# Linear attention with decay, then an MLP: three loads issued earlier, two groups of stores later, and a state sum moved ahead of the normalised rows

## The chip, the cores and the metric

One core of one Trainium2 chip. The metric is the device time in microseconds of one execution, as the median over several; lower is better. The engines are TensorE (PE; its weight loads are shown as PEld), VectorE (DVE), ScalarE (ACT), GpSimd (POOL) and SyncE (SP, which here only issues transfers; rows of an engine's queue carry a q, as in SPq).

## What is computed

Causal linear attention with a decay `lam` per head, in blocks of 64 positions with a running state, and on its output a layer norm and an MLP with a residual. The input is float32: q, k and v of 4 batches, 8 heads, 768 positions, 64 wide; the model width is 512, the hidden width 2048.

```python
for b in range(nb):                      # 12 blocks of 64 positions
    intra = einsum('bhic,bhjc->bhij', qb, kb) * Dmask[None]
    intra = einsum('bhij,bhjd->bhid', intra, vb)
    inter = einsum('bhid,bhde->bhie', qb * lam_pow[None], kv_state)
    out[:, :, sl] = intra + inter
    kv_state = lam_block * kv_state + einsum('bhsd,bhse->bhde', kb * rev_pow, vb)
xn = (x - mean(x)) / sqrt(var(x) + 1e-06) * g_ln     # x: heads side by side
out = x + maximum(xn @ w_ch1, 0.0) @ w_ch2
```

## The kernel before

**The pieces.** The 3072 rows (4 batches of 768) are cut into twelve *pairs* u = 0 to 11 of 256 rows; a pair is two chunks of 128 rows, piece of sequence u // 4 of batch u % 4. What the change calls the eighth pair is u = 7, and so on. Pairs 0 to 5 hold the score matrix of a whole chunk (functions `kv`, `scores`, `mask`, `av`), pairs 6 to 11 that of 64 positions (`kv64`, `scores64`, `mask64`, `states64`, `av64`).

**The way of one pair.** SP loads k, q and v (`load_in`, issued at L76 as one transfer for pairs below 6 and at L80 as two of 256 KB from pair 6 on). `in_k_one` (L231) casts k to bfloat16, `in_q_one` (L236) multiplies q by powers of lam, `in_v` (L242) does that to v; each `_one` call does half, on the engine that it is given. `transpose_dma` (L257) has the transposes of k and q made by a transfer that SP issues. PE makes the state terms pk (L324 or L389) and the scores (L279 or L370); DVE masks the scores (mA, L289 or L376). DVE adds pk to the old state (Stmp, L334, or Smid and Stmp, L405 and L408) and POOL multiplies the sum by the decay and writes the new state Sn (L330). PE multiplies scores by v (`av`, L436 or L423) and q by the state (`inter`, L449). `norm` reads the result: ACT copies it to x and takes its sum and mean (L475, L476), DVE writes the normalised rows x' (xc, L477). `to_xT` transposes x' for the MLP: on PE for pairs 2 to 4 (L510, copied by ACT at L511), else by a transfer from SP (L503). The MLP's first product is L547 (two chunks at once) or L658 (one), its relu on ACT (hT, L550 or L661). From group 4 on the second product is made with seven products in place of eight: DVE forms sums of hidden rows (`h_sums`: hs, L565 to L567) and the products go to four banks pwa to pwd (L582); they are scaled and added into x by ACT and POOL (L606 and L607, L614 and L615) and by DVE (L595). `rstd_of` is L520, L521 and L525; the earlier groups use L684 and L708. `store` (L716) writes a pair's rows in two transfers from SP.

**The two states of a pair.** `new_state(u, 0, ...)` adds pk0 to the batch's old state and has POOL make Sn; `new_state(u, 1, ...)` adds pk1 to that new Sn and has POOL make the next. So the second sum reads what POOL made of the first.

**What sets the order.** Nothing reorders the work: the program text is the schedule. Every engine runs its instructions in the order in which the text records them, and waits at an instruction for what it reads or overwrites. The MLP of earlier pairs is a list of units; `units(n)` records the next n of them between the steps of the attention. So the text from L1100 on is a long list of steps such as `load_in(8, "k", nc.sync)`, `units(1)`, `X(7)`. `Y(u)` and `X(u)` are pieces that hold pair u's state and scores beside pair u - 1's output; `Y` is called for pairs 4 and 5 (the fifth and sixth), `X` for 6 to 11. In `Y`, DVE's order before the change is: first sum, first mask, the two rows of x', second sum, three masks.

**Buffers.** PSUM has one tag "mm" of four banks, shared by pk, early scores, the MLP's first product and the second product's accumulators; a bank is free when its reader is done. k, q and v have three buffers each for what is loaded (inp), kq and its transposes three, vb four, x six; x is overwritten by the MLP's result and is free when its store has landed. SP's transfers share eight semaphores, so that each waits for the transfer eight before it.

Of the kernel before, what the change touches and what calls it, by code (L numbers as in the profile page):

```python
# [17 lines left out]
def kernel(  # L18
# [11 lines left out]
    nc = tc.nc  # L30
# [41 lines left out]
    def fill(got, name, u, hs, eng=None):  # L72
        eng = eng or nc.sync
        src = dict(k=k, q=q, v=v)[name]
        if u < LB:
            eng.dma_start(got[:, hs], source(src, u, hs))  # L76
            return
        cc, b = divmod(u, B)
        for j in range(2):
            eng.dma_start(got[:, hs, j * D:(j + 1) * D],  # L80
                          src[b, hs, cc * W + j * C:cc * W + (j + 1) * C, :].rearrange("h p d -> p h d"))
# [11 lines left out]
    def load_in(u, name, eng):  # L93
        got = qkv_in[u][name]
        fill(got, name, u, slice(0, H), eng)
        qkv_in[u][name] = got.rearrange("p h (j d) -> p h j d", j=2)
# [101 lines left out]
    def open_window(u):  # L198
        kq = wk.tile([128, 2, NP, 2, 2, D], BF16, tag="kq", bufs=3, name="kq")
        vb = wk.tile([128, H, 2, D], BF16, tag="vb", bufs=4, name="vb")  # L200
        st[u] = dict(kq=kq, vb=vb)
        if u < XB:
            st[u]["kqT"] = wk.tile([128, 2, NP, 2, 128], BF16, tag="kqT", bufs=3, name="kqT")

    def part(a, dst, hs):

        return dst[:, a, hs.start // 2:hs.stop // 2].rearrange("p a j e d -> p a e j d")
# [21 lines left out]
    def in_k_one(u, eng, j):  # L229
        src = qkv_in[u]["k"].rearrange("p (a e) j d -> p a e j d", e=2)  # L230
        (eng.copy if eng is nc.scalar else eng.tensor_copy)(part(0, st[u]["kq"], ALL)[:, :, :, j], src[:, :, :, j])  # L231

    def in_q_one(u, eng, j):
        src = qkv_in[u]["q"].rearrange("p (a e) j d -> p a e j d", e=2)
        lq = (lam_q[:, :, j] if u < LB else lam_p[:, 0, :]).rearrange("p (a e) -> p a e", e=2)
        eng.tensor_tensor(part(1, st[u]["kq"], ALL)[:, :, :, j], src[:, :, :, j],  # L236
                          lq[:, :, :, None].to_broadcast([128, NP, 2, D]), op=ALU.mult)

    def in_v(u, eng, hs=ALL):
        n = hs.stop - hs.start  # L240
        lv = lam_v[:, hs, :, None] if u < LB else lam_p[:, 1, hs, None, None]
        eng.tensor_tensor(st[u]["vb"][:, hs], qkv_in[u]["v"][:, hs], lv.to_broadcast([128, n, 2, D]), op=ALU.mult)  # L242
# [10 lines left out]
    def transpose_dma(u, a):  # L253
        s = st[u]
        if "kqT" not in s:
            s["kqT"] = wk.tile([128, 2, NP, 2, 128], BF16, tag="kqT", bufs=3, name="kqT")
        nc.sync.dma_start_transpose(s["kqT"][:, a].rearrange("p b j t -> p (b j) t"),  # L257
                                    s["kq"][:, a].rearrange("p b j e d -> p (b j e d)"))
# [26 lines left out]
    def mask(u, hf, heads=(0, 1)):  # L285
        s = st[u]
        kp = keep.rearrange("p a b t -> p a (b t)")
        for e in heads:
            nc.vector.tensor_tensor(s[f"mA{hf}"][:, e], s[f"sc{hf}"][e],  # L289
                                    kp[:, None, :, :].to_broadcast([128, 2, 2, 128]), op=ALU.mult)  # L290
# [38 lines left out]
    def decay(eng, dst, src):  # L329
        eng.tensor_tensor(dst, src, lam_s[:, :, None].to_broadcast([128, NP, D]), op=ALU.mult)  # L330

    def state_sum(u, ab):
        tmp = wk.tile([128, NP, D], F32, tag="Stmp", name="Stmp")
        nc.vector.tensor_tensor(tmp, st[u]["pk"][ab], state[u % B], op=ALU.add)  # L334
        return tmp

    def new_state(u, ab, eng):

        s = st[u]
        b = u % B  # L340
        if ab == 1 and len(s["pk"]) == 1:
            return
        old = state.get(b)
        if ab == 0:
            s["S"] = [(old, old)]
        Sn = wk.tile([128, NP, D], BF16, tag="S", bufs=12, name="Sn")
        if old is None and eng is nc.scalar:
            for p in range(NP):
                nc.scalar.activation(Sn[:, p], s["pk"][ab][:, p], ACT.Identity, scale=lam_s[:, p:p + 1])
        elif old is None:  # L350
            decay(nc.vector, Sn, s["pk"][ab])
        else:
            tmp = s.pop("tmp", None) or state_sum(u, ab)
            decay(eng, Sn, tmp)
        state[b] = Sn
        if ab == 0:
            s["S"].append((Sn, Sn))
# [97 lines left out]
    def reader(u, act=False):  # L455
        s = st[u]
        for ab in range(2):
            if s["S"][ab][1] is not None:
                seen = wk.tile([128, H], F32, tag="seen", name="seen")
                (nc.scalar.copy if act or u > WG else nc.vector.tensor_copy)(seen, s["po"][ab][:, :, 0])  # L460

    def norm(u, ab, early=False):
        s = st[u]
        po = s["po"][ab].rearrange("p h d -> p (h d)")
        if "x" not in s:
            s["x"] = xp.tile([128, 2, DM], F32, tag="x", bufs=6, name="x")
            s["mv"] = xp.tile([128, 2, 2], F32, tag="mv", name="mv")
            s["xc"] = wk.tile([128, 2, DM], BF16, tag="xc", name="xc")
        x, mv, xc = s["x"][:, ab], s["mv"][:, ab], s["xc"][:, ab]
        if u >= 2:  # L470
            if ab == 0:
                s["sum"] = xp.tile([128, 2], F32, tag="sum", name="sum")
                s["nmean"] = xp.tile([128, 2], F32, tag="nmean", name="nmean")
            sm, nm = s["sum"][:, ab:ab + 1], s["nmean"][:, ab:ab + 1]
            nc.scalar.activation(x, po, ACT.Copy, accum_out=sm)  # L475
            nc.scalar.activation(nm, sm, ACT.Copy, scale=-1.0 / DM)  # L476
            nc.vector.scalar_tensor_tensor(xc, in0=po, scalar=nm, in1=g_row, op0=ALU.add, op1=ALU.mult)  # L477
            return
        if not early:
            nc.scalar.copy(x, po)  # L480
        stats = wk.tile([128, 6], F32, tag="stats", name="stats")
        nc.vector.bn_stats(stats, po if early else x)
        nc.vector.bn_aggr(mv, stats)
        n_h = 2 if u == 0 else 1
        for h in range(n_h):
            sl = slice(h * DM // n_h, (h + 1) * DM // n_h)
            nc.vector.scalar_tensor_tensor(xc[:, sl], in0=po[:, sl], scalar=mv[:, 0:1], in1=g_row[:, sl],
                                           op0=ALU.subtract, op1=ALU.mult)
# [205 lines left out]
    def rows_of(u):  # L694

        cc, b = divmod(u, B)
        order = "(c p j) d -> j p c d" if u < LB else "(j c p) d -> j p c d"
        return out[b, cc * W:(cc + 1) * W, :].rearrange(order, c=2, j=2)
# [15 lines left out]
    def store(u):  # L714
        for j in range(2):
            nc.sync.dma_start(rows_of(u)[j], o_of[u][half[j]])  # L716
# [222 lines left out]
    def Y(u):  # L939
        kv(u)  # L940
        av(u - 1, range(NP))
        inter(u - 1, 0, fence=False)
        reader(u - 1, act=True)
        scores(u, 0)
        scores(u, 1, early=True)
        inter(u - 1, 1)
        new_state(u, 0, nc.gpsimd)
        mask(u, 0, (0,))
        norm(u - 1, 0)
        norm(u - 1, 1)  # L950
        new_state(u, 1, nc.gpsimd)
        mask(u, 1)
        mask(u, 0, (1,))

# [102 lines left out]
    def units(n):  # L1057
        for _ in range(n):
            f, *a = next(steps)
            f(*a)  # L1060
# [76 lines left out]
    load_in(6, "v", nc.sync)  # L1137
    units(1)
    Y(4)
    transpose_dma(5, 0)  # L1140
    transpose_dma(5, 1)
# [24 lines left out]
    open_in(8, False)  # L1166
    units(4)
    Y(5)
    transpose_dma(6, 1)
    units(1)  # L1170
    in_q_one(7, nc.gpsimd, 0)
    units(1)
# [6 lines left out]
    rstd_of(4)  # L1179
    units(2)  # L1180
    in_k_one(7, nc.vector, 1)
    load_in(7, "v", nc.sync)
    load_in(8, "k", nc.sync)
    in_v(7, nc.gpsimd)
    units(1)
    in_k_one(7, nc.scalar, 0)
# [2 lines left out]
    units(1)  # L1189
    X(6, rest=False)  # L1190
    open_window(8)
    store(1)
    store(2)
    transpose_dma(7, 0)
    transpose_dma(7, 1)
    to_xT(5, 0)
    to_xT(5, 1)
    units(3)
# [2 lines left out]
    open_in(9, False)  # L1201
    units(1)
    in_k_one(8, nc.gpsimd, 0)
    units(2)
    in_k_one(8, nc.vector, 1)
    units(1)
    load_in(8, "q", nc.sync)
    load_in(8, "v", nc.sync)
    units(1)
    rstd_of(5)  # L1210
    units(3)
    units(1)
    X(7)
    in_q_one(8, nc.gpsimd, 0)
    in_q_one(8, nc.gpsimd, 1)
    load_in(9, "k", nc.sync)
    units(1)
    in_v(8, nc.gpsimd)
    units(1)
# [33 lines left out]
    transpose_dma(9, 0)  # L1253
    to_xT(7, 1)
    units(2)
    store(3)
    units(2)
    m2s[6].sums(0, 4)
    m2s[6].sums(4, 8)
    units(3)  # L1260
    store(4)
    load_in(10, "q", nc.sync)
    units(3)
    rstd_of(7)
    units(1)
# [114 lines left out]
```

## Time and profile before

| | us |
|---|---|
| median of 3 runs (lowest, highest) | 209.29 (208.67, 210.65) |
| the profiled execution | 209.5 |
| its span, first to last instruction | 207.8 |
| granted TensorE clock over it | 1.00 |
| ACT busy, share of the span | 122.5, 59% |
| POOL busy, share of the span | 84.9, 41% |

The span is that of one execution; 1.7 us of its time lie around it. Times in the text such as "at 69.53" are microseconds from the start of the span. In a row of groups or of the timeline, `out<-in` names what an instruction writes and reads, a number in brackets at the end is how long its engine had been idle before it, and the name behind the arrow what ended that. A row of waits gives the sum in us, the number of waits and the longest. The shares of the transfer engines by fortieths of the span:

```
DMA  4999999999899799999698789899999020058403
```

Each digit is a slice of 5.2 us, in tenths: the transfer engines are busy nearly throughout until about 160 us.

### The profile page before, as it was taken

The numbers are of one execution on the slowest core, as the hardware profiler recorded it, in microseconds if no ns is written. First come the engines' busy times: TensorE is split into PE (matmuls) and PEld (weight loads), VectorE is DVE, ScalarE is ACT, GpSimd is POOL, SyncE is SP. The second block draws the span as 40 slices with busy tenths as digits, with TensorE's granted clock in tenths as the row PEclk, the third lists the DMA queues.
The fourth block names the chain that finished last, engine by engine and source line by source line (L and its number), as shares of the span: only waits on it lengthen the run. The fifth ranks groups of instructions, "written<-read, shape, count | busy, mean of one in ns | idle before, by whom it ended". The sixth has DMA issues, their size and how long they took to land.

```text
span 207.8 us, 7500 instructions
## 1 busy us (share of the span) xinstructions
PE 197.0 (95%) x3229; PEld 159.8 (77%) x3229; DVE 137.5 (66%) x274; ACT 122.5 (59%) x284; POOL 84.9 (41%) x117
## 2 busy tenths in 40 slices
PE   1999999999999999997999999999999999999992
PEld 0588888454775686686888899887888888888881
DVE  3588451647875665859979874748877957865253
ACT  3787678435443575774575775584596575652630
POOL 5657059118674604535248361753265202002020
PEclk9999999999999999999999999999999999999999
DMA  4999999999899799999698789899999020058403
GB/s 111 301 252 221 183 266 169 200 293 270 214 201 284 180 159 216 175 229 233 110 236 123 167 179 168 181 256 131 210 165 203 6 51 3 17 122 276 148 6 97
DMA packets 91011, 36.41 MB, mean 175 GB/s; under 512 B 65121, under 2 KB 88161, under 8 KB 90978
## 3 DMA queue, kind: packets, MB, share of 16 engines
q1 hardware_dynamic: 86368, 31.53, 72.9%
q0 software_dynamic: 4224, 4.19, 12.9%
q8 instruction: 25, 0.41, 0.9%
q10 hardware_dynamic: 386, 0.20, 0.4%
q14 instruction: 8, 0.07, 0.1%
HBM read 27.27 MB, written 6.29 MB: 162 GB/s over the span
## 4 chain that ended last, share of the span: by engine, by line
PE 47%; DMA 27%; DVE 9%; POOL 8%; SPq 3%; issue 2%; ACT 1%; POOLq 0%; DVEq 0%; ACTq 0%
PE pm L547 20%; DMA w<-in_moe_w_ch_dram 11%; DMA qin<-in_q_dram 6%; PE pwd L582 5%; DMA kin<-in_k_dram 5%; PE pwc L582 5%; DMA vin<-in_v_dram 5%; PE pwa L582 5%; PE pm L684 3%; PE pm1t L658 3%; POOL vb L242 3%; DVE hs L567 2%; PE pwb L582 2%; DVE hs L565 2%; DVE x L595 2%
## 5 line engine op out<-in xcount | busy, mean ns | idle before, releaser
L547 PE MATMUL pm<-xT,w 128*128 128x256 bf16 x640 | 73.7, 273 | 0.2 <-DVE Stmp L334 0.2
L547 PEld LDWEIGHTS <-w 128*128 128x128 bf16 x640 | 61.4, 98 | 8.6 <-DVE Stmp L334 0.7
L550 ACT ACTIVATE hT<-pm 128x512 f16<-128x512 f32 x80 | 47.0, 597 | 25.1 <-PE pm L547 24.6
L684 PE MATMUL pm<-w,hT 128*128 128x512 f16 x128 | 29.6, 379 | 0.0
L582 PEld LDWEIGHTS <-hs 128*128 128x128 f16 x256 | 24.8, 98 | 3.9 <-DVE hs L565 1.0
L607 POOL TENSOR_TENSOR x<-ev_u,x 128x256 f32<-128x256 f32 x8 | 6.3, 787 | 42.9 <-ACT ev_u L606 31.5
L565 DVE TENSOR_TENSOR hs<-hT 128x1024 f16<-128x1024 f16 x16 | 11.3, 704 | 15.9 <-ACT hT L550 13.9
L684 PEld LDWEIGHTS <-hT 128*128 128x128 f16 x128 | 11.9, 98 | 12.6
L330 POOL TENSOR_TENSOR Sn<-Stmp,lam_s 128x256 bf16<-128x256 f32 x16 | 9.9, 622 | 27.4 <-DVE Stmp L408 19.8
L582 PEld LDWEIGHTS <-hT 128*128 128x128 f16 x192 | 18.7, 98 | 2.1
L658 PE MATMUL pm1t<-xT,w 128*128 128x128 bf16 x256 | 16.4, 223 | 1.9 <-DVE Smid L405 1.5
L658 PEld LDWEIGHTS <-w 128*128 128x128 bf16 x256 | 15.6, 101 | 2.6 <-DVE Smid L405 1.7
L242 POOL TENSOR_TENSOR vb<-vin,lam_p 128x1024 bf16<-128x1024 f32 x6 | 11.7, 1946 | 11.0 <-DMA vin<-in_v_dram 11.0
L475 ACT ACTIVATE x<-po 128x512 f32<-128x512 f32 x18 | 10.6, 590 | 8.5 <-PE po L449 5.1
L477 DVE SCALAR_TENSOR_TENSOR xc<-po,nmean,g_row 128x512 bf16<-128x512 f32 x18 | 12.9, 745 | 3.1 <-ACT nmean L476 2.8
L242 POOL TENSOR_TENSOR vb<-vin,lam_v 128x1024 bf16<-128x1024 f32 (+1 forms) x7 | 11.6, 1662 | 5.1 <-DMA vin<-in_v_dram 5.0
L661 ACT ACTIVATE hT<-pm1t 128x512 f16<-128x512 f32 x16 | 9.6, 598 | 6.5 <-PE pm1t L658 6.5
L520 ACT ACTIVATE sq<-x,nmean 128x512 bf16<-128x512 f32 x18 | 12.9, 719 | 0.3
L567 DVE TENSOR_TENSOR hs<-hs,hT 128x512 f16<-128x512 f16 x16 | 11.9, 746 | 0.6
L236 POOL TENSOR_TENSOR kq<-qin,lam_p 128x512 bf16<-128x512 f32 x9 | 9.7, 1093 | 2.0 <-DMA qin<-in_q_dram 2.0
L595 DVE SCALAR_TENSOR_TENSOR x<-pwd,rstd,x 128x256 f32<-128x256 f32 x16 | 7.7, 482 | 3.2 <-POOL x L615 3.2
L595 DVE SCALAR_TENSOR_TENSOR x<-pwa,rstd,x 128x512 f32<-128x512 f32 (+1 forms) x16 | 9.1, 613 | 0.7
(137 smaller groups left out, 325.5 us busy)
## 6 DMA issues: line engine op xcount, KB each, us to landing
out_dram<-x SPq DMA_DIRECT2D x22, 256.0 KB, 4.1
w<-in_moe_w_ch_dram POOLq DMA_DIRECT2D x8, 512.0 KB, 8.3
kin<-in_k_dram SPq DMA_DIRECT2D x14, 256.0 KB, 4.9
qin<-in_q_dram SPq DMA_DIRECT2D x14, 256.0 KB, 4.6
vin<-in_v_dram SPq DMA_DIRECT2D x14, 256.0 KB, 5.3
kin<-in_k_dram SPq DMA_DIRECT2D x5, 512.0 KB, 6.4
qin<-in_q_dram SPq DMA_DIRECT2D x5, 512.0 KB, 7.8
vin<-in_v_dram SPq DMA_DIRECT2D x5, 512.0 KB, 9.8
```

The lines of the kernel that those rows point to most:

```text
L242: eng.tensor_tensor(st[u]["vb"][:, hs], qkv_in[u]["v"][:, hs], lv.to_broadcast([128, n, 2, D]), op=ALU.mult)
L475: nc.scalar.activation(x, po, ACT.Copy, accum_out=sm)
L477: nc.vector.scalar_tensor_tensor(xc, in0=po, scalar=nm, in1=g_row, op0=ALU.add, op1=ALU.mult)
L520: nc.scalar.activation(sq, s["x"][:, ab], ACT.Square, bias=s["nmean"][:, ab:ab + 1], accum_out=ss[:, ab:ab + 1])
L547: nc.tensor.matmul(pm[:, b, :], lhsT=w1[n // W2K][:, kk, (n % W2K) * 128:(n % W2K + 1) * 128], rhs=xT_of[g][:, kk, 0:N], start=(b == 0 and ...
L550: nc.scalar.activation(hT[:, u * NB:(u + 1) * NB, 0:N], pm, ACT.Relu)
L565: nc.vector.tensor_tensor(s13, b[:, :, 1:2, :].to_broadcast([128, n, 2, 128]), b[:, :, 0:4:3, :], op=ALU.subtract)
L567: nc.vector.tensor_tensor(s4, s2, b[:, :, 2], op=ALU.add)
L582: nc.tensor.matmul(pr[bank], lhsT=lhs(r), rhs=rhs, start=(first and r == 0), stop=(r == KB // 2 - 1), skip_group_check=True)
L595: nc.vector.scalar_tensor_tensor(out, in0=in0, scalar=r[ab], in1=in1, op0=ALU.mult, op1=ALU.add)
L658: nc.tensor.matmul(pm[:, b, :], lhsT=w1[c][:, kk, b * 128:(b + 1) * 128], rhs=xT_of[g][:, kk, i * 128:(i + 1) * 128], start=(b == 0 and kk ...
L684: nc.tensor.matmul(acc[i], lhsT=hT[:, kk, i * 128:(i + 1) * 128], rhs=w2[kk // W2K][:, kk % W2K, :], start=(kk == 0), stop=(kk == KB - 1))
```

## The change

Six edits, none of which adds or removes an instruction.

- In `Y` (pairs 4 and 5) the second state sum and POOL's state behind it, `new_state(u, 1, nc.gpsimd)`, stand ahead of the two `norm` calls of pair u - 1 instead of behind them.
- v of pair 7 is issued behind the first of pair 6's two transposes, instead of behind both, and behind other steps, ahead of k of pair 8.
- q of pair 8 is issued directly behind k of pair 8, ahead of pair 7's transposes, instead of ahead of v of pair 8. Its two products on POOL, `in_q_one(8, nc.gpsimd, ...)`, stand among the steps between `X(6)` and `X(7)` instead of behind `X(7)`: the first behind POOL's cast of k, the second behind POOL's two additions L607 and L615.
- The stores of pairs 1 and 2 (four transfers) stand behind pair 7's two transposes instead of ahead of them.
- k of pair 9 is issued by a line ahead of `X(7)` instead of one behind it. On SP it stands behind v of pair 8 in both.
- q of pair 10 is issued ahead of the stores of pairs 3 and 4 (four transfers) instead of behind them.

```diff
 def Y(u):
     ...
     mask(u, 0, (0,))
+    new_state(u, 1, nc.gpsimd)
     norm(u - 1, 0)
     norm(u - 1, 1)
-    new_state(u, 1, nc.gpsimd)
     mask(u, 1)
     mask(u, 0, (1,))
...
     Y(5)
     transpose_dma(6, 1)
+    load_in(7, "v", nc.sync)
     units(1)
     in_q_one(7, nc.gpsimd, 0)
     units(1)
...
     in_k_one(7, nc.vector, 1)
-    load_in(7, "v", nc.sync)
     load_in(8, "k", nc.sync)
+    load_in(8, "q", nc.sync)
     in_v(7, nc.gpsimd)
...
     X(6, rest=False)
     open_window(8)
+    transpose_dma(7, 0)
+    transpose_dma(7, 1)
     store(1)
     store(2)
-    transpose_dma(7, 0)
-    transpose_dma(7, 1)
     to_xT(5, 0)
     to_xT(5, 1)
...
     in_k_one(8, nc.gpsimd, 0)
+    in_q_one(8, nc.gpsimd, 0)
     units(2)
     in_k_one(8, nc.vector, 1)
     units(1)
-    load_in(8, "q", nc.sync)
+    in_q_one(8, nc.gpsimd, 1)
     load_in(8, "v", nc.sync)
+    load_in(9, "k", nc.sync)
     units(1)
     rstd_of(5)
     units(3)
     units(1)
     X(7)
-    in_q_one(8, nc.gpsimd, 0)
-    in_q_one(8, nc.gpsimd, 1)
-    load_in(9, "k", nc.sync)
     units(1)
     in_v(8, nc.gpsimd)
...
     units(2)
+    load_in(10, "q", nc.sync)
     store(3)
     units(2)
     m2s[6].sums(0, 4)
     m2s[6].sums(4, 8)
     units(3)
     store(4)
-    load_in(10, "q", nc.sync)
```

## The prediction

> **What bounds the kernel now.** I read the page's busy times first, then who waited for whom on TensorE, then timelines around the moved lines, then SP's queue.
>
> ```profile
> PE 197.0 (95%) x3229; PEld 159.8 (77%) x3229; DVE 137.5 (66%) x274; ACT 122.5 (59%) x284; POOL 84.9 (41%) x117
> ```
>
> TensorE (PE) is busy 95% of 207.8 us, in an order written by hand, so the time falls only by what PE idles and rises by whatever makes PE wait. PE's waits:
>
> ```profile
> PE g_all L180 <- DMA g_one<-in_moe_g_ln_dram: 4.2, 1, 4.2
> PE pm1t L658 <- DVE Smid L405: 1.5, 1, 1.5
> PE pwc L582 <- DVE hs L565: 0.4, 1, 0.4
> ```
>
> The first is the start. The other two are about all that is to be won behind it. First, the place of the changed function Y, its call Y(4), POOL, then DVE, then PE:
>
> ```profile
> 67.02 1.90 POOL L242 TENSOR_TENSOR vb<-vin,lam_v 128x1024 bf16<-128x1024 f32 x1 [2.46 <-DMA vin<-in_v_dram]
> 68.88 0.61 POOL L330 TENSOR_TENSOR Sn<-Stmp,lam_s 128x256 bf16<-128x256 f32 x1
> ```
> ```profile
> 65.51 0.69 DVE L289 TENSOR_TENSOR mA<-sc,keep 128x512 bf16<-128x512 f32 x1 [0.22 <-PE sc L279]
> 66.34 1.56 DVE L477 SCALAR_TENSOR_TENSOR xc<-po,nmean,g_row 128x512 bf16<-128x512 f32 x2
> 69.53 0.42 DVE L334 TENSOR_TENSOR Stmp<-pk,Sn 128x256 f32<-128x256 f32 x1 [1.63 <-POOL Sn L330]
> 69.87 1.28 DVE L289 TENSOR_TENSOR mA<-sce,keep 128x512 bf16<-128x512 f32 x2
> ```
> ```profile
> 68.38 0.61 PE L510 MATMUL xt<-ident,xc 128*128 128x128 bf16 x8
> 68.82 1.03 PE L684 MATMUL pm<-w,hT 128*128 128x512 f16 x4
> 70.01 5.41 PE L547 MATMUL pm<-xT,w 128*128 128x256 bf16 x48 [0.16 <-DVE Stmp L334]
> ```
>
> See the order on DVE: x' (xc, L477) runs at 66.34, PE transposes it at 68.38, and only then does DVE wait 1.63 us for the first state Sn, which stands on POOL behind a v product that had waited for its load. Second, the stall in X(6), in the same order of engines:
>
> ```profile
> 91.83 1.96 POOL L242 TENSOR_TENSOR vb<-vin,lam_p 128x1024 bf16<-128x1024 f32 x1 [3.80 <-DMA vin<-in_v_dram]
> ```
> ```profile
> 91.61 0.42 DVE L566 TENSOR_TENSOR hs<-hs,hT 128x512 f16<-128x512 f16 x1
> 92.07 2.00 DVE L567 TENSOR_TENSOR hs<-hs,hT 128x512 f16<-128x512 f16 x1
> ```
> ```profile
> 96.14 1.07 PE L658 MATMUL pm1t<-xT,w 128*128 128x128 bf16 x16 [1.53 <-DVE Smid L405]
> ```
>
> L567, alike in form to L566, takes 2.00 us instead of 0.42: it ends 0.28 us after the POOL product beside it. The state sums behind it, which free PE's bank, are late by that. Third, the same with q of the eleventh pair:
>
> ```profile
> 140.96 0.83 DVE L236 TENSOR_TENSOR kq<-qin,lam_p 128x512 bf16<-128x512 f32 x1 [3.23 <-DMA qin<-in_q_dram]
> ```
> ```profile
> 143.97 0.61 PE L582 MATMUL pwc<-wt,hs 128*128 128x256 f16 x4 [0.42 <-DVE hs L565]
> ```
>
> Last, SP's queue, which from 62 to 103 us issues almost without a pause:
>
> ```profile
> 81.48 4.65 SPq L257 DMA_TRANSPOSE kqT<-kq  x2
> 86.19 1.24 SPq L80 DMA_DIRECT2D vin<-in_v_dram  x2
> 94.18 3.91 SPq L257 DMA_TRANSPOSE kqT<-kq  x2
> 98.19 3.49 SPq L503 DMA_TRANSPOSE xT<-xc  x2
> ```
>
> **The change part by part.** No instruction is added or removed; all is order.
>
> 1. Second state sum ahead of x', in Y(4). The sum needs Sn, which POOL ends at 69.50 (68.88 + 0.61); nothing ahead of it is moved, so it still starts at 69.53. But now x' is queued behind it on DVE, and PE's transposes wait for x'. The next DVE instruction starts 0.34 after the sum (69.87 today), so x' runs 69.87 to 70.62 and, at the 0.67 spacing of two such in a row (1.40 for two elsewhere), 70.54 to 71.29. The second four transposes start at 71.35; four take 0.22 (eight: 68.38 to 68.82), so L684 starts at 71.57 instead of 68.82 and L547 0.86 later at 72.43 instead of 70.01: **+2.4**. Ends: +2.2 (if ACT's and PE's handovers overlap more) to +2.7 (x' at 0.81 spacing, as today). Behind x' wait three masks and L708; they end by 74.2, before q of the seventh pair lands (74.45), which DVE needs next: nothing more.
> 2. The same in Y(5): Sn is ready at 82.48, the mask ends at 82.72, and DVE then idles 0.72 until x' has its mean. The sum (0.42) fits: **0**. Cover gone, it would be 0.42. POOL's second Sn comes 2 us sooner, and with it q's products of the eighth pair (L236, 85.98); no one waits for them.
> 3. v of the eighth pair, moved ahead of one transpose on SP. The first transpose ends at 84.8, so v issues about 84.8 to 86.0 instead of 86.19 to 87.43, and lands, at today's 4.2, near 90.2. Its product takes 1.9 on POOL: 90.3 to 92.2. The transpose it passes slips 1.2; its reader stands at 91.98 + 2.4, four us behind its landing: 0. The sums of hidden rows (L565 to L567) start when ACT is done, 90.88 + 2.4 = 93.3, so the product is over: L567 costs 0.43, 1.57 less, and the bank is free 0.1 after PE wants it. Today PE goes on at 96.14 instead of 94.45: **-1.6**. Ends: 0 (product still beside the sums) to -1.7.
> 4. q of the ninth pair, issued before the transposes of the eighth pair, and its two products (1.04 each) on POOL in X(6)'s tail instead of X(7). POOL: the k cast ends at 98.2 today, then q's product follows at once, beside L565 to L567 of the second half (97.88). DVE waits as L567 did: L566 ends 0.3 after the product, L567 0.3 after L607 on POOL (0.8), then the k cast L231 after the second q product. That puts the eviction L595 of pwd near 103.2 in today's times, and the last product into pwd wants it at 102.29: +0.9. On SP, q adds two issues (0.6 each or more) and the four stores now stand behind the transposes; x' transposes (xT of the sixth pair) end 1.2 to 2.3 later than today's landing at 102.79, PE wants them at 103.16, 0.8 later by items 1 and 3, so this waits 0 to 1.1; it is the same PE time as the eviction's wait, so the larger counts, not both. I take **+0.8**; ends 0 (nothing collides and the transfer queue has room) to +1.2.
> 5. With q's products gone from X(7), POOL's v product of the ninth pair starts when the states are done, and L566 (1.15) and L567 (2.00) at 110 to 113 shrink; PE's stretch of eight pwc, 1.28 instead of 1.04, loses its wait: **-0.2** (0 to -0.24). k of the tenth pair is issued behind v as today; its readers come at 115: 0.
> 6. q of the eleventh pair ahead of two stores (four issues, 132.36 to 135.42): it lands 3 us sooner, about 137, before DVE gets to it (137.73). The sums then run when the hidden rows are there, and pwd follows pwc at 143.83 instead of 144.42: **-0.6** (0 to -0.6). The stores go 2 us later; the x buffers that they free are wanted at 149.4, some eight us after they land. The transpose behind them waits for POOL anyhow: 0.
> 7. Stores of the second and third pair behind two transposes: the first x buffer that they free is wanted by ACT's L475 at 118.9, some 18 us after they land: 0.
>
> A rule to weigh. The row: PE idles 1.53 us before 96.14, and sixteen pm1t then take 1.07, as the sixteen before them (1.06), so that gap cost no speed; at the start, at 16.55, sixteen took 1.68, with a granted clock of 1.00 shown all the same. Item 1 makes a gap of 2.1 us, and 3.0 with only eight transposes in it, longer than any such row. The sum by the row takes 0. The Trainium skill, "TensorE: Matmul & The Clock Gate", section "Part 1: The HAM clock gate", says that an idle window of about 3.4 us halves TensorE's clock, and its Part 4 that transposes do not count as busy as matmuls do. By that rule 3.0 us still is below the window, so 0 as well; were it reached, one slow window would cost an estimated 3.4 x 1/2 = 1.7 us and the sum would be +2.5. No run here shows it.
>
> **Sum.** +2.4 - 1.6 + 0.8 - 0.2 - 0.6 = +0.8 on the profiled execution's 209.5 (span 207.8): 210.3. That execution lies 0.2 above the median of the runs, 209.29; as a median I say 210.1.
>
> **The rivals.**
> - A: the stall in X(6) stays (item 3 gives 0): the product still meets the sums, because v lands after 92. For it: SP's issues stretch to 3.5 us at worst when the transfers are behind. Against: 2.4 us of delay moves the sums away from it. 210.1 + 1.6 = 211.7.
> - B: PE slows after the long gap. For it: the slow sixteen at the start. Against: 1.53 us did nothing. Price by the rows: 0.62 for each sixteen pm1t; over a stretch of 3 us (two issues of sixteen are 1.8) about 1.5: 211.6.
> - C, the other side: the v load of the sixth pair (62.18, landing 66.95) comes sooner, so that POOL is free when Sn is asked for (65.30). Then item 1 is near 0, but item 3 shrinks to -0.4, since the product (90.3 to 92.2) then holds up L565 at 90.88. Sum 0 - 0.4 + 0.8 - 0.2 - 0.6 = -0.4: 208.9, and 208.1 if item 4 is 0. It decides once Sn ends 0.8 us sooner, where item 1 falls below 1.6. Against: nothing ahead of that load is moved.
> - D: all loads were hidden anyhow and the swap too: 209.3. Against: PE follows DVE directly at 70.01.
>
> **How the numbers follow.** The forecast has 0.62, A 0.13, B 0.08, C 0.13, D 0.04. The forecast's own ends: 2.2 - 1.7 - 0.24 - 0.6 = -0.3 and 2.7 - 1.0 + 1.2 = +2.9 (with item 3 at -1.0 and items 5 and 6 at 0), not all at once. The range of 208.6 to 211.8 holds the forecast's middle, A, most of C and D. Within 1% (2.1 us, about what a measurement of this kernel can tell from no change) is 207.2 to 211.4. Slower by more: most of A, B and the forecast's upper tail, 0.20. Faster by more: C with nothing lost in item 4 and more won, 0.03. The rest, 0.77, is within 1%.
>
> **What would show it.** Right, step by step: DVE's Stmp in Y(4) ahead of xc with a wait of some 3 us for POOL's Sn, and PE's L510 waiting 2 us for xc (1); no wait of PE at Y(5) (2); L567 in X(6) at 0.43 and no PE wait there (3); L566 and L567 of the second half stretched, PE waiting for L595 or for xT (4); pwc and pwd without a wait near 114 and 144 (5, 6). Wrong: Sn ends before 68; L567 still at 2.0; sixteen pm1t behind the gap at 1.6.

## The result, and the profile after

The changed kernel took 211.35 us as the median of 20 executions (209.53 to 214.54), beside 208.73 for the kernel before (20 executions, 207.39 to 213.0): ratio 1.0115, 95% interval 1.0087 to 1.0142, so +2.4 us (1.8 to 3.0). A second measurement on one chip, told below, gave 1.0073 (1.0040 to 1.0106), +1.5. The forecast was +0.8. The profiled execution of the changed kernel took 210.42 us (span 208.7), 0.9 more than that of before. Nine of the changed kernel's 20 executions have a mean granted clock of 0.992 or less and a median of 213.59, beside 210.57 for the other eleven; the ratios leave most of those out, the medians do not.

The busy times of the changed kernel's page, then who waited for whom on TensorE:

```profile
PE 197.3 (95%) x3229; PEld 160.1 (77%) x3229; DVE 135.4 (65%) x274; ACT 122.4 (59%) x284; POOL 84.6 (41%) x117
```
```profile
PE g_all L180 <- DMA g_one<-in_moe_g_ln_dram: 4.2, 1, 4.2
PE xt L510 <- DVE xc L477: 1.7, 2, 1.4
PE pwd L582 <- DVE x L595: 0.7, 1, 0.7
PE pm1t L658 <- ACT xT L511: 0.3, 1, 0.3
PE pm L547 <- DMA xT<-xc: 0.2, 1, 0.2
```

PE's busy time is as before. The wait for Smid (1.5) and that before pwc (0.4) are gone; three have come: for x' (xc), for L595, and for the transposed x' (xT). DVE, then PE, around Y(4) in the changed kernel:

```profile
69.24 0.42 DVE L334 TENSOR_TENSOR Stmp<-pk,Sn 128x256 f32<-128x256 f32 x1 [2.60 <-POOL Sn L330]
69.58 1.40 DVE L477 SCALAR_TENSOR_TENSOR xc<-po,nmean,g_row 128x512 bf16<-128x512 f32 x2
```
```profile
66.21 2.76 PE L684 MATMUL pm<-w,hT 128*128 128x512 f16 x12
70.38 0.40 PE L510 MATMUL xt<-ident,xc 128*128 128x128 bf16 x4 [1.40 <-DVE xc L477]
71.04 0.40 PE L510 MATMUL xt<-ident,xc 128*128 128x128 bf16 x4 [0.26 <-DVE xc L477]
71.27 1.03 PE L684 MATMUL pm<-w,hT 128*128 128x512 f16 x4
72.13 0.60 PE L547 MATMUL pm<-xT,w 128*128 128x256 bf16 x4
```

The second sum now heads x', waits 2.60 us for Sn, and PE waits in two pieces. L547 comes at 72.13 instead of 70.01; 0.44 of that was there before Y(4), from the start of the kernel, which the change does not touch. In X(6), on DVE, POOL and PE of the changed kernel:

```profile
94.18 0.42 DVE L567 TENSOR_TENSOR hs<-hs,hT 128x512 f16<-128x512 f16 x1
...
99.31 1.15 DVE L566 TENSOR_TENSOR hs<-hs,hT 128x512 f16<-128x512 f16 x1
100.49 0.83 DVE L567 TENSOR_TENSOR hs<-hs,hT 128x512 f16<-128x512 f16 x1
...
102.24 0.95 DVE L231 CAST kq<-kin 128x512 bf16<-128x512 f32 x1
103.11 0.47 DVE L595 SCALAR_TENSOR_TENSOR x<-pwd,rstd,x 128x256 f32<-128x256 f32 x1
```
```profile
88.34 1.90 POOL L242 TENSOR_TENSOR vb<-vin,lam_p 128x1024 bf16<-128x1024 f32 x1 [0.49 <-DMA vin<-in_v_dram]
...
98.69 1.48 POOL L236 TENSOR_TENSOR kq<-qin,lam_p 128x512 bf16<-128x512 f32 x1
...
101.87 1.04 POOL L236 TENSOR_TENSOR kq<-qin,lam_p 128x512 bf16<-128x512 f32 x1
```
```profile
95.55 2.20 PE L658 MATMUL pm1t<-xT,w 128*128 128x128 bf16 x32
...
103.64 1.03 PE L582 MATMUL pwd<-w,hs 128*128 128x256 f16 x8 [0.66 <-DVE x L595]
104.85 1.03 PE L547 MATMUL pm<-xT,w 128*128 128x256 bf16 x8 [0.18 <-DMA xT<-xc]
```

The v product is over at 90.2, L567 takes 0.42 and the 32 pm1t run on without a break: the stall is gone. The two q products (L236) now stand beside L566 (1.15) and the k cast L231 (0.95), L595 of pwd ends at 103.58, 0.6 after PE ran out of work (it idles from 102.98), and PE waits once more for xT.

PE's instructions are the same 3229 in nearly the same order in the kernels below (gap_filled has seven more, which are left out), so two traces can be laid side by side instruction by instruction. How much PE lost (+) or won (-) in each stretch against the profiled execution of before, in us:

| kernel (profiled execution) | start | Y(4) | X(6) | pwd, xT at 103 | X(7) | pwd at 144 | sum with the rest |
|---|---|---|---|---|---|---|---|
| changed | +0.44 | +1.68 | -1.58 | +1.16 | -0.24 | -0.60 | +0.77 |
| changed, again | 0.00 | +1.76 | -1.58 | +2.15 | -0.24 | -0.59 | +1.33 |
| swap_only | +0.78 | +1.30 | -1.58 | 0 | 0 | +0.14 | +0.55 |
| loads_only | +0.61 | -0.09 | -1.57 | +2.19 | -0.24 | -0.59 | +0.29 |
| gap_filled | +0.21 | +1.99 | -1.58 | +0.82 | -0.24 | -0.59 | +0.40 |
| v_sooner | +0.23 | -0.09 | -1.58 | 0 | 0 | +0.13 | -1.39 |
| xT_ahead | -0.17 | +1.32 | -1.58 | +0.82 | -0.24 | -0.59 | -0.57 |
| products_back | +2.07 | +3.41 | -1.54 | +1.06 | -0.01 | -0.59 | +4.83 |
| gap_longer | +0.58 | +4.26 | -1.58 | +1.12 | -0.24 | -0.59 | +3.90 |
| v_q_sooner | +0.52 | -0.09 | -1.58 | 0 | 0 | -0.59 | -1.86 |
| v_behind | +1.18 | -0.09 | -1.58 | +1.64 | -0.24 | -0.60 | +0.28 |
| before, second profile | -0.10 | -0.09 | -0.81 | +0.45 | 0 | -0.09 | -0.60 |
| before, third profile | +0.01 | +0.05 | +0.10 | 0 | 0 | +0.17 | +0.14 |

The rest, in no column, is up to 0.3 in a kernel, and 0.55 behind Y(4) in gap_longer and 0.45 in products_back.

### The profile page after: what moved, and what is told of

It is laid out like the page before. It is cut to its first block, busy times and chain, and to the rows that moved or that the text cites. A ratio compares the mean times of both kernels' runs of the same rounds, so it can differ in the third digit from the quotient of the medians.

```text
span 208.7 us, 7501 instructions
## 1 busy us (share of the span) xinstructions
PE 197.3 (95%) x3229; PEld 160.1 (77%) x3229; DVE 135.4 (65%) x274; ACT 122.4 (59%) x284; POOL 84.6 (41%) x117
## 4 chain that ended last, share of the span: by engine, by line
PE 73%; DMA 12%; DVE 4%; POOL 3%; ACT 3%; issue 2%; SPq 1%; POOLq 0%; ACTq 0%; DVEq 0%
PE pm L547 29%; PE pm1t L658 7%; PE pm L684 6%; PE pwd L582 5%; PE pwc L582 5%; PE pwa L582 5%; DMA vin<-in_v_dram 5%; DMA kin<-in_k_dram 4%; PE pwb L582 3%; PE tp L250 2%; POOL vb L242 2%; DMA xT<-xc 1%; PE po L449 1%; DMA g_one<-in_moe_g_ln_dram 1%; PE po L436 1%
## 5 line engine op out<-in xcount | busy, mean ns | idle before, releaser
L547 PE MATMUL pm<-xT,w 128*128 128x256 bf16 x640 | 73.6, 273 | 0.2 <-DMA xT<-xc 0.2
L547 PEld LDWEIGHTS <-w 128*128 128x128 bf16 x640 | 61.5, 98 | 8.5 <-issue 0.4
L684 PE MATMUL pm<-w,hT 128*128 128x512 f16 x128 | 29.6, 379 | 0.0
L565 DVE TENSOR_TENSOR hs<-hT 128x1024 f16<-128x1024 f16 x16 | 14.4, 897 | 17.2 <-ACT hT L550 14.7
L607 POOL TENSOR_TENSOR x<-ev_u,x 128x256 f32<-128x256 f32 x8 | 6.0, 746 | 47.2 <-ACT ev_u L606 35.8
L684 PEld LDWEIGHTS <-hT 128*128 128x128 f16 x128 | 11.9, 98 | 12.6
L236 POOL TENSOR_TENSOR kq<-qin,lam_p 128x512 bf16<-128x512 f32 x9 | 10.1, 1140 | 0.0
L595 DVE SCALAR_TENSOR_TENSOR x<-pwd,rstd,x 128x256 f32<-128x256 f32 x16 | 7.7, 482 | 3.6 <-POOL x L615 3.6
L595 DVE SCALAR_TENSOR_TENSOR x<-pwa,rstd,x 128x512 f32<-128x512 f32 (+1 forms) x16 | 9.1, 613 | 0.8
L289 DVE TENSOR_TENSOR mA<-sce,keep 128x512 bf16<-128x512 f32 x10 | 6.4, 683 | 4.9 <-PE sce L279 4.9
```

What stands on the lines that cost most here:

```text
L547: nc.tensor.matmul(pm[:, b, :], lhsT=w1[n // W2K][:, kk, (n % W2K) * 128:(n % W2K + 1) * 128], rhs=xT_of[g][:, kk, 0:N], start=(b == 0 and ...
L565: nc.vector.tensor_tensor(s13, b[:, :, 1:2, :].to_broadcast([128, n, 2, 128]), b[:, :, 0:4:3, :], op=ALU.subtract)
L595: nc.vector.scalar_tensor_tensor(out, in0=in0, scalar=r[ab], in1=in1, op0=ALU.mult, op1=ALU.add)
L684: nc.tensor.matmul(acc[i], lhsT=hT[:, kk, i * 128:(i + 1) * 128], rhs=w2[kk // W2K][:, kk % W2K, :], start=(kk == 0), stop=(kk == KB - 1))
```

## The experiments

The kernel before took 208.68 us (median) on the chip of the changed kernel's second measurement, swap_only, loads_only and gap_filled; 207.99 on that of before_look, v_sooner, xT_ahead and products_back; 208.23 on that of before_look2, gap_longer, v_q_sooner and v_behind. Ratios are against these.

**The changed kernel again.** Unchanged.

> The changed kernel once more, on the chip of the next three. Theory W (waits alone): the ratio to the kernel before is what the two profiles show, 209.5 to 210.4, so about 1.004, and the first measurement (1.0115) was high because single executions scatter. Theory K (the clock): the gap of PE at Y(4) lets PE's granted clock fall for one stretch in part of the executions, about 1.7 us in each of those; the ratio is again near 1.01, and the runs scatter more than those of the kernel before, with a mean clock near 0.992 in the long ones.

210.16 us, ratio 1.0073 (1.0040 to 1.0106). Between the two expectations: +1.5, more than the 0.9 that the two profiles differ by and less than the first +2.4. The mean granted clock was 0.992 or less in two of these 12 executions, in nine of the first 20, and in two of the 35 of the kernel before beside it.

**The swap alone.** The kernel before, with this:

```diff
+        new_state(u, 1, nc.gpsimd)
         norm(u - 1, 0)
         norm(u - 1, 1)
-        new_state(u, 1, nc.gpsimd)
```

> The kernel before with the two lines of Y alone swapped. W: L547 behind Y(4) comes 1.7 to 2.4 us later, and since the hidden-row sums in X(6) come later too, the product of v beside them is mostly over, so that the stall of 1.53 us there goes although v is loaded as before: +0.3 to +0.9 us in all, ratio 1.001 to 1.004. If the stall in X(6) goes only by the earlier load of v: +1.7 to +2.4, ratio 1.008 to 1.011, with L567 still at 2.0 us. K: the gap stands here too, so +1.5 to +2.5 with clocks near 0.992 in the long runs, although the profile shows no PE wait left in X(6).

210.65 us, ratio 1.0073 (1.0036 to 1.0110), +1.5. Two rows of DVE in this kernel:

```profile
93.80 0.43 DVE L566 TENSOR_TENSOR hs<-hs,hT 128x512 f16<-128x512 f16 x1
94.26 0.43 DVE L567 TENSOR_TENSOR hs<-hs,hT 128x512 f16<-128x512 f16 x1
```

The profile answers as W said, with a somewhat smaller delay: +1.30 at Y(4), and the delay alone takes the stall of X(6) away, though v is loaded as before. The time answers as the reading without that gain: +1.5, as if nothing were won at X(6). K's low clocks are there too, at or below 0.992 in five of the 12 executions, but they do not make the +1.5: the other seven have a median of 210.18, still 1.5 over the kernel before. A gain that the traces show and the times do not have points at the execution that it is counted from; two more profiles of before, below, are for that.

**The moves without the swap.** The changed kernel, with this:

```diff
-        new_state(u, 1, nc.gpsimd)
         norm(u - 1, 0)
         norm(u - 1, 1)
+        new_state(u, 1, nc.gpsimd)
```

> The changed kernel with the old order in Y: all moves of loads, products and stores, no swap. W and K alike: no gap at Y(4), 0 there; the product of v then meets the first hidden-row sums of X(6) (about 90 to 92 us), so item 3 gives 0.4 in place of 1.6; with +0.8 to +1.2 (item 4), -0.2 and -0.6 the sum is -0.4 to 0, ratio 0.998 to 1.000, and the runs scatter no more than those of the kernel before. Rival: if the loads and stores moved are what made the changed kernel's executions long (transfers colliding), this one stays near 1.01.

209.6 us, ratio 1.0033 (0.9996 to 1.0070), +0.7. All the moves together win nothing, with or without the swap. Item 3 gave its whole 1.57 in the trace, not 0.4: v landed by 88.7, so its product was over before the sums began at 91.56. And item 4 cost 2.19, nearly three times its forecast; PE's waits in this kernel:

```profile
PE pm L547 <- DMA xT<-xc: 1.2, 1, 1.2
PE pwd L582 <- DVE x L595: 0.7, 1, 0.7
```

Without the delay at Y(4), PE comes to xT 1.4 us earlier than in the changed kernel's first profile, the last xT lands 0.4 sooner (104.42, not 104.81), and PE waits longer for it. But that date moves by itself: in the changed kernel's second profile it is 105.53 and the wait 1.2 as here, so that the missing delay makes the difference is not shown.

**Y(4)'s gap filled.** The changed kernel, with products of zero weights:

```diff
     units(3)
+    m2s[2].add_zero(7)
     to_xT(3, 0)
```

> The changed kernel with seven products of zero weights (128x512, some 0.22 us each, 1.5 us in all), added to an accumulator of the MLP's second product just ahead of Y(4)'s transposes, so that PE idles 0.1 to 0.6 us there in place of 2.1 and everything else is as in the changed kernel. They add nothing to the result. W: same time as the changed kernel beside it (between 0 and +0.3 us). K: the long executions go, the median comes down by 1 to 1.7 us against the changed kernel beside it, and no run shows a mean clock near 0.992.

210.1 us, ratio 1.0078 (1.0044 to 1.0112); the changed kernel beside it 210.16. The seven products ran in what had been idle time (line numbers are higher here; L694 is the added product, L512 the transposes):

```profile
68.59 1.67 PE L694 MATMUL pm<-w,zero 128*128 128x512 f16 x7
70.46 0.40 PE L512 MATMUL xt<-ident,xc 128*128 128x128 bf16 x4 [0.19 <-DVE xc L479]
```

W holds: the same time, to within the 0.7 us of the interval, so on this chip it was the wait's length, not the clock, that made the changed kernel slower. K's fall of the median by 1 to 1.7 us did not come; that the low clocks go did: no execution of 12 had a mean clock below 0.995, where the unfilled kernel had two at 0.992.

**Two more profiles of the kernel before.** Unchanged, one execution each.

> The kernel before once more, unchanged, for a second profile of it. Theory S: the stall of 1.53 us in X(6) belongs to every execution, so L567 takes about 2.0 us again and PE waits 1.3 to 1.7 us for Smid. Theory N: it depends on when v of the eighth pair happens to land, and in most executions it is small: L567 at 0.4 to 1.2, PE waiting less than 0.8.

> The kernel before, unchanged, for a third profile. The two so far show PE waiting 1.53 and 0.8 us for Smid in X(6). Theory N (the stall comes and goes with the landing of v): anything from 0 to 1.5, and the execution's time lower by as much as the stall is smaller. Theory S (it is in every execution): 1.3 to 1.7 again, and the 0.8 was the exception.

208.91 and 209.62 us. PE's wait for Smid in the second profile, then in the third:

```profile
PE pm1t L658 <- DVE Smid L405: 0.8, 1, 0.8
```
```profile
PE pm1t L658 <- DVE Smid L405: 1.7, 1, 1.7
```

Two of the three profiles show the stall in full. In the second profile it has another form: the v product started at 91.92, just behind L567, and held up POOL's Sn instead (a wait of 0.90 on DVE):

```profile
91.87 0.43 DVE L567 TENSOR_TENSOR hs<-hs,hT 128x512 f16<-128x512 f16 x1
...
94.65 0.42 DVE L405 TENSOR_TENSOR Smid<-pk,Sn 128x256 f32<-128x256 f32 x1 [0.90 <-POOL Sn L330]
```

It comes and goes, as N said; the second profile's 0.8 is outside S's 1.3 to 1.7, though no profile was without a stall. All three executions lie above the kernel's medians: 209.5 against 208.73, 208.91 against 207.99, 209.62 against 208.23, and of the 23 executions beside the third profile eleven took 206.97 to 208.09.

**v of the eighth pair alone.** The kernel before, with this:

```diff
     transpose_dma(6, 1)
+    load_in(7, "v", nc.sync)
...
     in_k_one(7, nc.vector, 1)
-    load_in(7, "v", nc.sync)
```

> The kernel before with v of the eighth pair alone loaded sooner. S: 1.57 us less, as the profile of the kernel with all loads moved shows between 90 and 96 us: ratio 0.992 to 0.993. N: the profile shows no wait in X(6), but there was little to win in most executions: ratio 0.997 to 1.000. The prediction's rival C (the product meets the first sums, since nothing delays them here): 0.4 us less, ratio 0.998, with L565 near 92 stretched and PE still waiting about 1.1 us.

208.08 us, ratio 0.9990 (0.9956 to 1.0024). POOL, then DVE in this kernel:

```profile
88.24 1.90 POOL L242 TENSOR_TENSOR vb<-vin,lam_p 128x1024 bf16<-128x1024 f32 x1
```
```profile
91.14 0.69 DVE L565 TENSOR_TENSOR hs<-hT 128x1024 f16<-128x1024 f16 x1 [0.72 <-ACT hT L550]
92.32 0.42 DVE L567 TENSOR_TENSOR hs<-hs,hT 128x512 f16<-128x512 f16 x1
```

PE's trace shows no wait in X(6) and 1.58 won there against the first profile; the times show 0.2, and at most 0.9. The times refute S; the trace refutes C's variant (the product was over at 90.1, ahead of the sums, and L565 took 0.69). That the median execution of before has little of this stall follows from the times; it is an inference, since no profile fell on such an execution.

**The stores behind the x' transposes.** The changed kernel, with this:

```diff
-    store(1)
-    store(2)
     to_xT(5, 0)
     to_xT(5, 1)
+    store(1)
+    store(2)
```

> The changed kernel with the stores of pairs 1 and 2 behind the sixth pair's x' transposes instead of ahead of them. Theory T (on SP, four stores and q of the ninth pair now stand ahead of these transposes, which therefore land 1.5 to 2 us later than before): they are issued by 98.5, PE's wait for xT (0.2 and 1.2 us in the two profiles of the changed kernel) goes, the wait for L595 (0.7) stays: 0.2 to 1.2 less, about 0.7 less than the changed kernel, ratio to the kernel before about 1.005. Theory P (only the products of q on POOL cost): same as the changed kernel, about 1.008, xT not sooner or not waited for.

SP's queue in the changed kernel, then in this one:

```profile
92.49 2.62 SPq L257 DMA_TRANSPOSE kqT<-kq  x2
95.16 4.28 SPq L716 DMA_DIRECT2D out_dram<-x  x4
99.55 3.65 SPq L503 DMA_TRANSPOSE xT<-xc  x2
```
```profile
91.52 2.82 SPq L257 DMA_TRANSPOSE kqT<-kq  x2
96.80 2.50 SPq L503 DMA_TRANSPOSE xT<-xc  x2
99.36 4.16 SPq L716 DMA_DIRECT2D out_dram<-x  x4
```

The trace is T's: xT is issued 2.75 us sooner, PE no longer waits for it, and the stretch costs 0.82, all of it the wait for L595. The time does not bear it out: 209.4 us, ratio 1.0097 (1.0061 to 1.0132), above the 1.005 expected, and no better than the changed kernel's 1.0073 and 1.0115 in other measurements. T stands by the trace alone.

**The q products back.** The changed kernel, with this:

```diff
-    in_q_one(8, nc.gpsimd, 0)
...
-    in_q_one(8, nc.gpsimd, 1)
...
     X(7)
+    in_q_one(8, nc.gpsimd, 0)
+    in_q_one(8, nc.gpsimd, 1)
```

> The changed kernel with the two products of q of the ninth pair back behind X(7); loads and stores as in the changed kernel. T: the wait for L595 goes, but the x' transposes land when they did, so PE waits for them 0.7 longer: nothing won there, and the 0.2 of item 5 lost again, ratio about that of the changed kernel to 0.001 over it (1.008 to 1.010). P: 0.7 to 1.2 less where PE waited for L595 and 0.2 more at X(7), ratio about 1.004.

211.53 us, ratio 1.0120 (1.0056 to 1.0183, six executions). One of PE's waits:

```profile
PE pm L547 <- DMA xT<-xc: 0.9, 1, 0.9
```

T again: PE's wait for L595 is gone, a wait of 0.9 for xT stands in its place, so the stretch still costs 1.06; and item 5 falls from -0.24 to -0.01, which confirms that term. The profiled execution was a long one (214.39), and by chance shows what rival B spoke of. Columns of the next two fences: the stretch and its length, then busy time of PE, its weight loads, DVE, ACT and POOL (instructions), the granted clock, DMA share and GB/s. This kernel, from 69.32 on:

```profile
69.32:72.73 3.41, 1.30 (x7) 0.40 (x5) 1.15 (x3) 0.00 (x0) 2.84 (x3) 1.00 1.01 228
72.73:76.14 3.41, 3.36 (x16) 1.80 (x17) 2.79 (x5) 1.69 (x3) 0.61 (x1) 0.50 1.09 224
76.14:79.55 3.41, 3.41 (x33) 3.06 (x32) 3.41 (x4) 1.83 (x4) 2.11 (x1) 1.00 1.07 208
```

The clock is 0.50 for one stretch of 3.41 us behind one in which PE was busy 1.30.

**A longer gap.** The changed kernel, with this:

```diff
     in_v(5, nc.gpsimd)
+    in_v(5, nc.gpsimd)
```

> The changed kernel with the sixth pair's v product, which stands ahead of Y(4)'s states on POOL, made twice (the same product written again: 1.9 us more on POOL, same result), so that PE idles about 4 us ahead of and within Y(4)'s transposes in place of 2.1. Theory K (the granted clock is set anew every 3.41 us, to a half after a stretch of that length in which PE was busy less than about four tenths, as one profile shows): the clock is 0.5 for one stretch of 3.41 us right behind the gap in nearly every execution, mean clock 0.992 or less, and the time is 1.9 + 1.0 to 1.7 = 2.9 to 3.6 us over the changed kernel, ratio 1.022 to 1.028. Theory W (the gap costs its length alone): +1.9, clock 1.00, ratio 1.016 to 1.020.

213.4 us, ratio 1.0231 (1.0167 to 1.0295): K's number, above W's 1.016 to 1.020 though W's upper end lies in the interval. The clock decides: at or below 0.992 in four executions of four, and the profile has the same picture:

```profile
69.15:72.57 3.42, 0.40 (x4) 0.23 (x4) 1.63 (x3) 0.05 (x1) 2.88 (x4) 1.00 0.98 203
72.57:75.98 3.41, 3.24 (x14) 1.79 (x15) 2.79 (x6) 1.64 (x3) 0.97 (x2) 0.50 1.09 230
```
```profile
72.08 0.40 PE L510 MATMUL xt<-ident,xc 128*128 128x128 bf16 x4 [2.97 <-DVE xc L477]
72.74 0.61 PE L510 MATMUL xt<-ident,xc 128*128 128x128 bf16 x4 [0.26 <-DVE xc L477]
73.14 1.91 PE L684 MATMUL pm<-w,hT 128*128 128x512 f16 x4
```

Four L684 take 1.91 here and 1.03 in the changed kernel. Y(4) and the stretch to 90 cost 4.26 + 0.55 in place of 1.68: 3.1 more, 1.9 of it by length the doubled product, and the remaining 1.2 is put down to the clock.

**Only the two loads that should help.** The kernel before with v_sooner's edit and this:

```diff
     units(2)
+    load_in(10, "q", nc.sync)
     store(3)
...
-    load_in(10, "q", nc.sync)
```

> The kernel before with only v of the eighth pair and q of the eleventh pair loaded sooner: the changed kernel without the swap in Y, without q of the ninth pair's move, and with the stores of pairs 1 and 2 where they were. N: v gives 0 to 0.3 of the median, q 0.6: ratio 0.995 to 0.998, and the profile shows no wait in X(6) and none before pwd near 144. S: v gives 1.57, q 0.6: ratio 0.989 to 0.990. If neither was on the path: 1.000.

207.44 us, beside 208.23 for before: ratio 0.9986 (0.9956 to 1.0016). In the trace both gains are there, 1.58 and 0.59, and PE has no wait above 0.3 left behind the start; the times show 0.3 to 0.8 and do not exclude nothing. It is the lowest median of the study.

**The v product behind the states.** The changed kernel, with this:

```diff
-    in_v(5, nc.gpsimd)
...
     Y(4)
+    in_v(5, nc.gpsimd)
```

> The changed kernel with the sixth pair's v product behind Y(4)'s states on POOL instead of ahead of them; the swap stays. If item 1's cost is POOL's order (the state waits for a product that waits for its load), the second sum finds Sn ready, PE's wait for xc goes, and the time is that of the changed kernel without the swap: ratio 1.001 to 1.005, with the waits for L595 and xT near 103 as there (together 1.2 to 2.2 us). If the swap costs by itself, through the sum's 0.42 us and x' behind it: 0.4 of the 1.7 stays. If the swap's cost has another cause: 1.007 to 1.012, as the changed kernel.

DVE in this kernel:

```profile
67.30 0.41 DVE L334 TENSOR_TENSOR Stmp<-pk,Sn 128x256 f32<-128x256 f32 x1
67.63 1.45 DVE L477 SCALAR_TENSOR_TENSOR xc<-po,nmean,g_row 128x512 bf16<-128x512 f32 x2
```

In the trace the mechanism is settled: with Sn early the sum waits for nothing and Y(4) costs -0.09, so the swap by itself is free and its 1.7 is POOL's order. The time is a miss: 209.9 us, ratio 1.0074 (1.0044 to 1.0104), not 1.001 to 1.005, though the interval overlaps that of loads_only, whose trace has the same Y(4). Its profile sums to +0.28 against before's; from an execution of before without the stall that would be about +1.9, of which 1.18 is a late start. Whether its late start is chance stays open.

## Why the prediction was right, and where it was not

The time lay in the range, and within 1% as its likeliest case had it by the second measurement, just above by the first. Part of that is luck: the forecast's middle, +0.8, lies below both intervals (the second begins at 1.0040), and item 1, too large by some 0.7, hid part of what items 3 and 4 lacked. By its own steps:

- **Item 1, +2.4 in Y(4): right in mechanism, over-sized.** Sum, wait for Sn, x' and the two groups of transposes stand as foretold; the cost was 1.30 to 1.76 in the four profiles that have the gap as it is and ran it at full clock, below the end of 2.2. The estimate fixed Sn's end at 69.50; here DVE had it at 69.24, though PE was 0.44 later by then. Sn hangs on the landing of v, which is not a constant: its product, in the same place of the text, began at 65.76 in xT_ahead and at 69.08 in products_back.
- **Item 2, 0 in Y(5): right.** The second sum stands at 84.75 and x' at 85.55, where it waited for its mean; PE waited for nothing.
- **Item 3, -1.6: right against the profiled execution, the failing step against the median.** The stretch shows -1.58 (v came 2 us sooner than estimated: its product ran from 88.34, not 90.3). But swap_only and v_sooner both lift it alone, so it was not item 3's to give beside item 1; and v_sooner, which does nothing else, changed the measured time by 0.2 (up to 0.9). The prediction took a stall of one profiled execution for one of every execution and put the sum back onto the median with a correction of 0.2.
- **Item 4, +0.8: the mechanism right, one term too small.** Both waits that it named came, L595's and xT's, and the larger counts, as it said: PE waits for L595 ahead of pwd, and behind it only for what is left of xT's lateness. Without xT's the stretch costs 0.82 (xT_ahead), without L595's 1.06 (products_back), with both 1.16. L595's +0.9 was about right; xT's 0 to 1.1 was too small. The stretch cost 0.82 to 1.16 with the gap at Y(4), 2.15 in one execution, 1.64 and 2.19 without the gap, so the bound of 1.2 was passed. xT_ahead shows what delays xT: the four stores ahead of it on SP.
- **Item 5, -0.2, item 6, -0.6: right**, -0.24 and -0.59, the first also by products_back, the second in all kernels that have the move. **Item 7, 0:** the x buffers were not waited for, but the stores have a cost, the one in item 4.
- **Rival A** (stall stays) and **D** (nothing) did not come. **C** did not in the profiled execution, where Sn ended 0.3 sooner and C needed 0.8. In xT_ahead's it ended at 68.23, 1.3 sooner, and item 1 was 1.32, below C's 1.6; but item 3 stayed at -1.58, not -0.4. **B** came in part: the clock fell in some executions, not at Y(4) in the profiled one. (The slow sixteen at 16.55, on which B rested, began before the clock first rose in that profile, at 17.85; sixteen like them at 19.58 took 1.05.) It does not explain the ratio of 1.0073, since gap_filled removed the fall and not the time; of the first measurement's 1.0115, with nine low clocks in 20, it may hold a part, since the median of the other eleven, 210.57, is 1.8 us above the 208.73 of before. loads_only, which has no gap at Y(4), had five low clocks in 12; its two waits near 103 would be the place, but no profile shows such an execution.

The size, then: item 1 about 1.7, item 4 about 1.2 to 2.2, items 5 and 6 with the rest -1.0, item 3 -0.2 as v_sooner measured it, together +1.7 to +2.7. Measured were +1.5 and +2.4. The forecast's +0.8 lacks mainly item 3's 1.4.

The rule that was weighed, of the Trainium skill, "TensorE: Matmul & The Clock Gate", section "Part 1: The HAM clock gate (the "warmup" mystery)", puts the halving behind an idle window of about 3.4 us. The length agrees with 3.41 here. The page also calls the window free-running, which fits the different first rises below. But the window need not be idle: 1.30 us of work in it did not prevent the fall, so the estimate that 3.0 us was safe was not.

## What to carry to other kernels

Before a stall is counted as a gain, look at it in two or three executions and see where the profiled one lies among the times; a wait that hangs on when a load lands is not in every one. Two edits that cure the same wait are counted once. When a step moves ahead of a queue's reader, list what the readers behind it then wait for, on the engine and on the transfer queue, as dates rather than lengths: a delay upstream can hide them, and its removal show them again. Such a date is itself uncertain (104.81 and 105.53 for xT in two executions of one kernel).

## What the runs showed of the hardware

- TensorE's clock was granted anew in steps of 3.413 us. In every trace the stretches at full clock were whole multiples of it (16 and 40 of them in products_back and gap_longer, 55 to 58 elsewhere), counted from where the clock first rose (11.8 to 18.9 us, different in each execution). It fell to 0.5 behind a step with PE busy 0.38 (products_back) and 0.12 (gap_longer) of the time, and once more around the end of every execution, as PE's work ran out: in the changed kernel behind 0.41 (203.25 to 206.66), which is why its mean is 0.995. It did not fall behind 0.50 (the kernel before, 202.17 to 205.58) nor behind any busier step; the lowest ahead of the end is 0.52, at the stall of before's third profile:

```profile
94.35:97.76 3.41, 1.76 (x28) 1.53 (x26) 3.14 (x7) 1.70 (x6) 1.88 (x5) 1.00 1.01 196
97.76:101.17 3.41, 3.41 (x34) 3.05 (x32) 3.31 (x7) 1.86 (x5) 2.00 (x4) 1.00 1.00 144
```

  So a gap of 2.1 us within one step was enough (products_back). The changed kernel's profile has 1.4 and 0.3 us of idling, spread over two steps (0.66 and 0.85 busy), and no fall there; how long the gap was in its nine executions with a low clock, no trace shows. PE's busy time is modelled, so the shares are rough.
- The start, the same in all these kernels up to 60 us but for one small fill in gap_filled, moved PE by -0.17 to +2.07 us between executions, mostly in waits for the weights' transfers. That alone is larger than most single terms of this change.
